# Loading a first-layer weight in two groups, deriving one sine table from the other, and one ring of PSUM banks in the set-up of a fused FFT and MLP-mixer kernel

## The chip, the cores and the metric

The kernel runs on one core of one Trainium2 chip. The metric is the device time of one execution in microseconds (us). One execution is also recorded by the profiler; its "span" runs from the first to the last instruction and is about 1.8 us shorter than the time of the same execution (609.8 against 611.57 us before the change).

Names used below: PE is the matrix engine, DVE the vector engine, ACT the scalar engine, POOL the engine that here issues most loads, SP the engine that issues stores and transposing DMAs. PEld, in the tables, is PE's loading of weights. PSUM is the memory that PE writes its products into. The "granted clock" is the share of full speed that the throttle lets PE run at.

## The reference, cut to what matters

```python
X = np.fft.fft(np.fft.fft(x, axis=1), axis=2).real        # x: 8 x 3008 x 256
xt = X.transpose(0, 2, 1)
h  = np.maximum(xt @ w_tok1, 0.0) @ w_tok2                 # token mixing, 3008 -> 256 -> 3008
u  = X + h.transpose(0, 2, 1)
out = u + np.maximum(u @ w_ch1, 0.0) @ w_ch2               # channel mixing, 256 -> 1536 -> 256
```

The kernel writes both Fourier transforms as products with sine tables that it generates itself. It folds the token transform into the first token weight once: the "carried" products hp and hq are w_tok1 multiplied by the transposed tables tp and tq. All batches then use hp and hq. So the set-up makes the tables, loads x of batch 0 and all the weights, and carries w_tok1 through the tables. After it comes a long steady part, 8 batches of 6 chunks.

## The kernel before: the parts that matter

The loads, all issued by POOL in this order: x of batch 0 (xp, xm), w_tok1 (w1p, w1m), w_tok2 (w2s), half of w_ch1 (wc1), later w_ch2 (wc2) and x of batch 1.

```python
    for i in range(2):                                   # w_tok1: four DMAs, 12 blocks each
        gdma(w1p[64 * i:64 * i + 64, :, :], dram(w1_t, ...))
        gdma(w1m[64 - 64 * i:128 - 64 * i, 0:NG - 1 + i, :], dram(w1_t, ...))
    w2s = const.tile([P, 2, S], FP16, tag="w2s")
    gdma(w2s[:], dram(w2_t, ...))
```

Each sine table is made from an angle reduced to one period: two ACTIVATEs (`near`) and one DVE operation (`rest_of`), then two sine ACTIVATEs (`table3`). The second table starts from its own angle, mq = mp + dq.

One carried product works on two blocks g, and reads both halves of the weight:

```python
    def carried(tts, dst, g2, e):
        ph = ps_mm("ph")
        for k in range(2):
            g = 2 * g2 + k
            o = ph[:, k * DTOK:(k + 1) * DTOK]
            nc.tensor.matmul(o, lhsT=tts[0][:, g * P:g * P + P], rhs=w1p[:, g, :],
                             start=True, stop=False)
            nc.tensor.matmul(o, lhsT=tts[1][:, g * P:g * P + P],
                             rhs=w1m[:, NG - 1 - g, :], start=False, stop=True)
        copy(e, dst[...], ph[:])          # e = 0: ACT, 1: DVE
```

PSUM has eight banks, kept in three pools: "mm" (3), "o2" (2) and "f" (3). The set-up interleaves three streams on PE, and the PE timelines below show them in this order (`own` yields eight groups of pz products and then twelve pw products of batch 0's transform):

```python
    take(own, 4)                         # the last four of the eight pz
    turn_rows(tts_p, 1.0, 0)             # "pr": rows of the first table reversed
    table3(tq, vq)                       # sines of the second table
    table_perm()
    take(own, 3)                         # pw 0 to 2
    carried(tts_p, hp, 0, 1)
    take(own, 2)
    carried(tts_p, hp, 1, 0)
    ...                                  # cut
    turn(tq, tts_q, 0)                   # "pt": the second table transposed
    ...                                  # cut: hp 3 to 5, hq 0 to 5, batch 0's token products
    filler(12)
    ...
        # steady part, first chunk; from batch 0's third step on:
                if b == 0 and 3 <= sub < 9:
                    take(early, 2)                       # fold of x of batch 1, on DVE
                    if sub == 8:
                        x_tiles[2] = load_x(2)
```

"pc" is the first product of the steady part (u times w_ch1). The time of the first pc marks the end of the set-up.

## Time and profile before

| | before |
|---|---|
| time, median of the runs beside the changed kernel (lowest to highest) | 611.77 us (611.5 to 613.0) |
| span of the profiled run, PE busy | 609.8 us, 97% |
| first pc | 38.56 us |
| PE waits for w1m | 2.15 us, until 21.64 us |
| granted clock between 21 and 25 us | 0.50 to 0.66 |

A kernel whose main engine is busy for 97% seems to leave little to gain. These are lines of the first two parts of its page: the span, busy time of PE, and then the span in 40 slices of about 15 us each, a digit being tenths of a slice.

```profile
span 609.8 us, 15701 instructions
...
PE 591.3 (97%) x6323; PEld 423.0 (69%) x6323; DVE 453.2 (74%) x1020; ACT 439.4 (72%) x986; POOL 147.8 (24%) x230
...
PE   5799999999999999999999999999999999999996
...
PEclk9899999999999999999999999999999999999999
```

PE is below 9 tenths only in the first two slices, some 30 us, and in the last, which this change does not touch. (The granted clock is below 9 in the second slice too.) A time by stretches shows the same: from 38.6 to 60 us PE is busy for 21.40 of 21.40 us. So only the first 38 us can give time back, as long as the change leaves the amount of steady work alone.

The chain of waits of the first 60 us (start, length, what; "issue" is time in which the engine waited for nothing that the profile shows), before the change:

```profile
6.33 0.86 POOL w1p L164
...
8.68 12.91 DMA w1m<-in_moe_w_tok_dram
21.59 0.04 issue
21.64 0.37 PE ph L403
```

The largest piece of the chain is 12.91 us in which the set-up depends on the last of the four w_tok1 loads. The PE timeline shows what that costs (start, length, engine, line of the program, operands, form, count; in brackets the idle time before it and who ended it):

```profile
17.17 0.23 PE L529 MATMUL pw<-tdu,z 128*128 128x128 f16 x1 [0.55 <-ACT z L288]
18.58 0.23 PE L529 MATMUL pw<-tdb,z 128*128 128x128 f16 x1 [1.18 <-DVE z L286]
...
19.22 0.27 PE L401 MATMUL ph<-w1p,tt 128*128 128x256 f16 x1
21.64 0.37 PE L403 MATMUL ph<-w1m,tt 128*128 128x256 f16 x1 [2.15 <-DMA w1m<-in_moe_w_tok_dram]
21.80 0.42 PE L401 MATMUL ph<-w1p,tt 128*128 128x256 f16 x1
...
36.72 1.33 PE L674 MATMUL pu<-w2s,uu 128*128 128x512 f16 x4 [0.73 <-ACT uu L605]
...
38.56 1.58 PE L714 MATMUL pc<-ut,wc1p 128*128 128x512 f16 x6
```

PE starts its first carried product at 19.22 us, because w1p is there, and stops at the second factor for 2.15 us. A stretch table of 1 us steps shows the other half of the cost (columns: window and its length; busy time of PE, PEld, DVE, ACT, POOL with counts; granted clock; DMA share; GB/s):

```profile
20.00:21.00 1.00, 0.00 (x0) 0.00 (x0) 0.06 (x1) 0.20 (x1) 1.00 (x3) 1.00 1.02 200
21.00:22.00 1.00, 0.36 (x2) 0.25 (x2) 0.00 (x0) 0.00 (x0) 0.50 (x2) 0.66 1.10 229
22.00:23.00 1.00, 1.00 (x11) 0.92 (x9) 0.53 (x1) 0.00 (x0) 0.39 (x1) 0.50 1.08 223
...
24.00:25.00 1.00, 1.00 (x11) 0.99 (x10) 0.01 (x1) 0.80 (x2) 0.00 (x0) 0.63 1.02 211
```

After the idle stretch, the clock is granted at half for about three microseconds. The ph products then start 0.21 us apart (21.80 to 22.02 us) instead of 0.11 us as later.

### The profile page before, as it was taken

The page shows a single profiled execution, that of the slowest core. Times are in us where ns is not written, and L with a number is a line of the kernel's source. Part 1 is how long each engine was busy: PE and PEld are TensorE (multiplying, and loading weights), DVE is VectorE, ACT ScalarE, POOL GpSimd, SP SyncE. Part 2 cuts the span into 40 slices and gives each one's busy share as a digit, 9 for nine tenths or more (in the row PEclk, how much of TensorE's full clock was granted, in tenths as well). Part 3 has the DMA queues.
Part 4 walks back from the last instruction along what each step waited for, and adds up shares of the span by engine and source line. Part 5 has one row for each costly group of instructions (what it writes and reads, how often), then busy time and mean ns, then how long its engine had stood idle before and what let it go on. Part 6 is the DMA issues. An engine that isn't in the chain of part 4 may idle for free.

```text
span 609.8 us, 15701 instructions
## 1 busy us (share of the span) xinstructions
PE 591.3 (97%) x6323; PEld 423.0 (69%) x6323; DVE 453.2 (74%) x1020; ACT 439.4 (72%) x986; POOL 147.8 (24%) x230
## 2 busy tenths in 40 slices
PE   5799999999999999999999999999999999999996
PEld 4566667666777678666777767766787667766675
DVE  8669679658987697757988689856979676676572
ACT  8666886677778777687777767777776877767772
POOL 8400413111143113401314212321131112111131
PEclk9899999999999999999999999999999999999999
DMA  9992953724538423682339333392231523232423
GB/s 153 209 185 81 185 75 59 152 50 85 67 74 153 90 53 68 115 125 53 78 63 168 61 81 77 64 185 58 53 68 45 100 53 78 64 70 59 90 58 100
DMA packets 86601, 56.53 MB, mean 93 GB/s; under 512 B 54864, under 2 KB 83472, under 8 KB 85776
## 3 DMA queue, kind: packets, MB, share of 16 engines
q1 hardware_dynamic: 78048, 37.84, 31.4%
q0 software_dynamic: 8256, 17.49, 16.6%
q8 instruction: 49, 0.80, 0.5%
q14 instruction: 24, 0.20, 0.1%
q10 hardware_dynamic: 224, 0.20, 0.1%
HBM read 34.98 MB, written 24.64 MB: 98 GB/s over the span
## 4 chain that ended last, share of the span: by engine, by line
PE 92%; DVE 3%; DMA 2%; ACT 1%; POOL 1%; issue 0%; DVEq 0%; POOLq 0%
PE pc L714 39%; PE px L755 23%; PE py L755 9%; PE pu L674 7%; PE po L812 4%; PE pt L582 4%; DMA w1m<-in_moe_w_tok_dram 2%; PE pz L486 1%; PE pq L614 1%; PE py L614 1%; PE pw L566 1%; PE pw L565 1%; DVE sb L731 1%; DVE w L568 1%; PE ph L403 0%; DVE osb L740 0%
## 5 line engine op out<-in xcount | busy, mean ns | idle before, releaser
L717 ACT ACTIVATE c<-pc 128x512 f16<-128x512 f32 (+1 forms) x572 | 295.8, 594 | 38.2 <-PE pc L714 20.6
L740 POOL TENSOR_TENSOR osb<-osb,rt 128x256 f32<-128x256 f32 x84 | 81.0, 964 | 381.3 <-DVE osb L740 364.8
L714 PE MATMUL pc<-ut,wc1p 128*128 128x512 f16 x576 | 140.5, 379 | 0.0
L755 PEld LDWEIGHTS <-c 128*128 128x128 f16 x2016 | 121.3, 98 | 20.7 <-issue 1.3
L714 PE MATMUL pc<-ut,wc1m 128*128 128x512 f16 (+1 forms) x576 | 134.8, 370 | 0.0
L682 DVE TENSOR_TENSOR ut<-pu,yt 128x512 f16<-128x512 f32 (+1 forms) x96 | 64.7, 674 | 52.9 <-PE pu L674 52.7
L755 PEld LDWEIGHTS <-sb 128*128 128x128 f16 x1512 | 89.9, 98 | 10.8 <-DVE sb L731 0.7
L760 ACT ACTIVATE m<-px 128x256 f32<-128x256 f32 x126 | 48.6, 386 | 66.9 <-PE px L755 41.9
L714 PEld LDWEIGHTS <-wc1p 128*128 128x128 f16 x576 | 52.2, 98 | 49.2 <-issue 2.6
L714 PEld LDWEIGHTS <-wc1m 128*128 128x128 f16 x576 | 53.0, 98 | 46.4
L755 PE MATMUL px<-wst,c 128*128 128x128 f16 x1008 | 70.8, 219 | 0.2 <-DVE c L731 0.2
L755 PE MATMUL px<-wc,c 128*128 128x128 f16 x1008 | 63.1, 219 | 0.0
L731 DVE TENSOR_TENSOR sb<-sb,c 128x768 f16<-128x768 f16 x84 | 50.3, 598 | 2.9
L288 ACT ACTIVATE z<-pz 128x480 f16<-128x480 f32 (+1 forms) x60 | 40.0, 671 | 16.9 <-PE pz L486 11.0
L740 DVE TENSOR_TENSOR osb<-py,m 128x256 f32<-128x256 f32 x84 | 35.2, 419 | 22.2 <-ACT m L760 17.4
L731 DVE TENSOR_TENSOR sb<-c 128x768 f16<-128x768 f16 x84 | 49.2, 586 | 2.4 <-ACT c L717 2.4
L674 PE MATMUL pu<-w2p,uu 128*128 128x512 f16 (+1 forms) x168 | 50.0, 379 | 0.0
L731 DVE TENSOR_TENSOR sb<-c,sb 128x768 f16<-128x768 f16 x84 | 47.1, 561 | 0.0
L731 DVE TENSOR_TENSOR c<-c 128x768 f16<-128x768 f16 x84 | 46.6, 554 | 0.0
L568 DVE SCALAR_TENSOR_TENSOR w<-alt,pw 128x131 f16<-128x131 f16 x84 | 29.4, 350 | 19.5 <-ACT w L288 18.9
L621 DVE TENSOR_TENSOR yt<-py,qs 128x512 f16<-128x512 f32 x48 | 30.9, 686 | 16.0 <-ACT qs L617 15.7
L755 PE MATMUL py<-wst,sb 128*128 128x128 f16 x504 | 35.2, 219 | 0.5 <-DVE sb L731 0.5
(186 smaller groups left out, 687.9 us busy)
## 6 DMA issues: line engine op xcount, KB each, us to landing
out_dram<-osb SPq DMA_DIRECT2D x83, 256.0 KB, 3.8
xp<-in_x_dram POOLq DMA_DIRECT2D x16, 272.0 KB
out_dram<-osb SPq DMA_DIRECT2D x11, 192.0 KB, 3.2
xp<-in_x_dram POOLq DMA_DIRECT2D x16, 127.5 KB
rt<-ut SPq DMA_TRANSPOSE x96, 3.5
w2s<-in_moe_w_tok_dram POOLq DMA_DIRECT2D x1, 1504.0 KB
w1p<-in_moe_w_tok_dram POOLq DMA_DIRECT2D x2, 384.0 KB
wc<-in_moe_w_ch_dram POOLq DMA_DIRECT2D x1, 768.0 KB
```

Of the source, the lines that this page charges most:

```text
L288: nc.scalar.activation(out=out_, in_=in_, func=AFT.Copy)
L568: nc.vector.scalar_tensor_tensor(out=w[:, g, 0:131], in0=alt[:], scalar=pw[:, 131:132], in1=pw[:, 0:131], op0=AT.mult, op1=AT.add)
L582: nc.tensor.matmul(pt[:, o:o + n], lhsT=hw[:, g, th * P:th * P + P], rhs=w[:, g, f:f + n], start=(g == 0), stop=(g == NG - 1))
L621: nc.vector.tensor_tensor(out=yt[:, h, CW * c:CW * c + CW], in0=py[:], in1=qs[:], op=op)
L674: nc.tensor.matmul(pu[:, 0:n], lhsT=uu[:, th, int(minus), h, :], rhs=w2_cols(b, c)[:, th], start=(th == 0), stop=(th == 1))
L682: nc.vector.tensor_tensor(out=ut[:, h, 0:n].rearrange("p (a b) -> p a b", b=64), in0=pu[:, 0:n].rearrange("p (b a) -> p a b", b=64), in1=y ...
L714: nc.tensor.matmul(pc[:, 0:n], lhsT=wc[:, h, ct * P:(ct + 1) * P], rhs=ut[:, h, 0:n], start=(h == 0), stop=(h == 1))
L717: nc.scalar.activation(out=c1[:, ct, 0:n], in_=pc[:, 0:n], func=AFT.Relu)
L731: nc.vector.tensor_tensor(out=o, in0=x, in1=y, op=op)
L740: eng.tensor_tensor(out=o, in0=x, in1=y, op=AT.add)
L755: nc.tensor.matmul(o[:, t], lhsT=a(k)[:, f:f + P], rhs=w(k), start=(first and t == 0 and k == 0), stop=(k == HC - 1), skip_group_check=True)
L760: nc.scalar.activation(out=m[:, i], in_=pa[:, 0], func=AFT.Copy)
```

## The change

The intent: begin the carried products with half of w_tok1 instead of waiting for all of it; make the second table available earlier and with less work on ACT; and let the set-up use all eight PSUM banks in turn, whatever stream asks. The diff, cut to its core:

```diff
+    ring = cycle((("f", 3), ("mm", 3), ("o2", 2), ("f", 3), ("mm", 3), ("f", 3), ("mm", 3),
+                  ("o2", 2)))
+    def ps_any(name, dt=FP32, n=512):
+        tag, bufs = next(ring)
+        return psum.tile([P, n], dt, tag=tag, name=name, bufs=bufs)
 ...   # pt, pr, fillers, ph, pz, pw and pt1 of the set-up take ps_any
-    for i in range(2):
-        gdma(w1p[64 * i:64 * i + 64, :, :], ...)
-        gdma(w1m[64 - 64 * i:128 - 64 * i, 0:NG - 1 + i, :], ...)
+    for g0, g1 in ((0, 6), (6, NG)):
+        for i in range(2):
+            gdma(w1p[64 * i:64 * i + 64, g0:g1, :], ...)
+            m0, m1_ = NG - g1, min(NG - g0, NG - 1 + i)
+            gdma(w1m[64 - 64 * i:128 - 64 * i, m0:m1_, :], ...)
 ...
-    nc.scalar.activation(out=mq[:], in_=mp[:], func=AFT.Identity, bias=dq[:])
+    nc.vector.scalar_tensor_tensor(out=vq[:], in0=vp[:], scalar=side[:], in1=vp[:],
+                                   op0=AT.mult, op1=AT.max)      # |vp| where side is -1
 ...   # four small DVE operations make side and the phase shifts; offq, dq and mq go
     warm(24)
-    near(vq, mq)
+    table3(tq, vq, (shift0[:], shift1[:]))
+    turn(tp, tts_p, 16)
     table_d()
     ...
-    rest_of(vq, mq, S)
 ...   # fillers, and which of ACT and DVE copies some products out of PSUM, change too
 ...   # order of the products after the folds of batch 0:
+    take(own, 3)
+    turned_out(tts_q, turn_in(tq))
+    for g2, e in enumerate((1, 1)):
+        carried(tts_p, hp, g2, e)
+    table_perm()
+    take(own, 4)
+    carried(tts_p, hp, 2, 0)
+    turn_rows(tts_q, -1.0, 0)
+    take(own, 3)
+    carried(tts_p, hp, 3, 1)
 ...
```

More of the change, by code (lines that the diff above doesn't have):

```diff
@@ L167 @@
     x_tiles = {0: load_x(0)}
-    icol, scol, gt32, eq32, mid, reff, offp, offq, tmp = (
+    icol, scol, gt32, eq32, mid, reff, offp, tmp = (
         pvec(n) for n in ("icol", "scol", "gt32", "eq32", "mid", "reff", "offp",
-                          "offq", "tmp"))
+                          "tmp"))
     ts(icol[:], pcol[:], 64.0, AT.is_ge)
@@ L189 @@
                                    op0=AT.mult, op1=AT.add)
-    nc.vector.scalar_tensor_tensor(out=offq[:], in0=mid[:], scalar=-752.0, in1=tmp[:],
-                                   op0=AT.mult, op1=AT.add)
-    for i in range(2):
-        gdma(w1p[64 * i:64 * i + 64, :, :],
-             dram(w1_t, i * DTOK, [[NQ * DTOK, 64], [2 * DTOK, NG], [1, DTOK]]))
-        gdma(w1m[64 - 64 * i:128 - 64 * i, 0:NG - 1 + i, :],
-             dram(w1_t, (25 - i) * DTOK,
-                  [[NQ * DTOK, 64], [2 * DTOK, NG - 1 + i], [1, DTOK]]))
+    for g0, g1 in ((0, 6), (6, NG)):
+        for i in range(2):
+            gdma(w1p[64 * i:64 * i + 64, g0:g1, :],
+                 dram(w1_t, (i + 2 * g0) * DTOK,
+                      [[NQ * DTOK, 64], [2 * DTOK, g1 - g0], [1, DTOK]]))
+            m0, m1_ = NG - g1, min(NG - g0, NG - 1 + i)
+            gdma(w1m[64 - 64 * i:128 - 64 * i, m0:m1_, :],
+                 dram(w1_t, (25 - i + 2 * m0) * DTOK,
+                      [[NQ * DTOK, 64], [2 * DTOK, m1_ - m0], [1, DTOK]]))
     w2s = const.tile([P, 2, S], FP16, tag="w2s")
@@ L238, in sin, with table3 @@
         nc.scalar.activation(out=out_, in_=in_, func=AFT.Sin, scale=PI2 / period)
-    def table3(tab, r):
+    def table3(tab, r, shift=(0.0, 0.0)):
         for i in range(2):
             nc.scalar.activation(out=tab[:, :, 64 * i:64 * i + 64], in_=r[:],
-                                 func=AFT.Sin, scale=half[i][:])
+                                 func=AFT.Sin, scale=half[i][:], bias=shift[i])
     def turned():
@@ L248, in turned, with turn_in @@
                 for _ in range(2)]
-    def turn(tab, tts, warm):
+    def turn_in(tab):
+        pts = []
         for h in range(2):
-            pt = psum.tile([P, 1024], FP16, tag="mm", name="pt", bufs=3)
+            pt = ps_any("pt", FP16, 1024)
             for g in range(6):
@@ L255, in turn, with turned_out @@
                                     in_=tab[:, 6 * h + g, :], identity=ident[:])
-            copy(0, tts[0][:, 768 * h:768 * h + 768], pt[:, 0:768])
+            pts.append(pt)
+        return pts
+    def turned_out(tts, pts):
+        for h in range(2):
+            copy(0, tts[0][:, 768 * h:768 * h + 768], pts[h][:, 0:768])
+    def turn(tab, tts, warm):
+        turned_out(tts, turn_in(tab))
         filler(warm)
@@ L260, in turn_rows @@
         for h in range(3):
-            pr = ps_mm("pr")
+            pr = ps_any("pr")
             nc.tensor.matmul(pr[:], lhsT=anti[:], rhs=tts[0][:, 512 * h:512 * h + 512],
@@ L272, in warm @@
     def warm(n):
-        pw = ps_out("filler")
+        pw = ps_any("filler")
         for _ in range(n):
@@ L278, in filler @@
     def filler(n):
-        pw = ps_mm("filler")
+        pw = ps_any("filler")
         for _ in range(n):
@@ L290 @@
     pl = nc.gpsimd
-    dq, r2, r47 = (pvec(n) for n in ("dq", "r2", "r47"))
-    nc.vector.tensor_tensor(out=dq[:], in0=offq[:], in1=offp[:], op=AT.subtract)
+    r2, r47 = (pvec(n) for n in ("r2", "r47"))
     ts(r2[:], reff[:], 2.0, AT.mult)
@@ L297 @@
     gp = gen.tile([P, NG], FP32, tag="gp")
-    mp, vp, mq, vq = (gen.tile([P, NG, 64], FP32, tag=n, name=n)
-                      for n in ("mp", "vp", "mq", "vq"))
+    mp, vp, vq = (gen.tile([P, NG, 64], FP32, tag=n, name=n)
+                  for n in ("mp", "vp", "vq"))
     ts(gp[:], jrow[:, 0:NG], r2[:], AT.mult, offp[:], AT.add)
@@ L321 @@
     ts(half[1][:], icol[:], PI2 / S, AT.mult)
+    quart, side, shift0, shift1 = (pvec(n) for n in ("quart", "side", "shift0", "shift1"))
+    nc.vector.tensor_tensor(out=quart[:], in0=gt32[:], in1=mid[:], op=AT.add)
+    ts(side[:], quart[:], -2.0, AT.mult, 1.0, AT.add)
+    for o, h in ((shift0, half[0]), (shift1, half[1])):
+        nc.vector.scalar_tensor_tensor(out=o[:], in0=h[:], scalar=-S / 4.0, in1=quart[:],
+                                       op0=AT.mult, op1=AT.mult)
     mask0, q24 = pvec("mask0"), pvec("q24")
@@ L394, with carried @@
     hq = const.tile([P, NG, DTOK], FP16, tag="hq")
-    def carried(tts, dst, g2, e):
-        ph = ps_mm("ph")
+    def carried(tts, dst, g2, e, pool=ps_any):
+        ph = pool("ph")
         for k in range(2):
@@ L513, in edge @@
                                  start=(i == 0), stop=(i == 1))
-        five = cycle((ps_f, ps_out, ps_f, ps_out, ps_f))
         for t0, e in Z0_ORDER:
@@ L518, in zw0 @@
                 if t0:
-                    inner(xp, t0, half, z_put(z, half, t0, e[half]), next(five))
+                    inner(xp, t0, half, z_put(z, half, t0, e[half]), ps_any)
                 else:
                     outer(xp, half, z_put(z, half, 0, e[half]), edge,
-                          next(five))
+                          ps_any)
                 yield
@@ L525, in zw0 @@
         for g in range(NG):
-            pw = next(five)("pw")
+            pw = ps_any("pw")
             for lo, hi in ((131, WD), (0, 131)):
@@ L536 @@
     Z0_ORDER = ((11, (0, 0)), (0, (1, 1)), (6, (0, 1)), (1, (0, 1)))
-    W0_COPY = [1] * 5 + [0, 1, 1, 1, 0, 1, 0]
+    W0_COPY = [1] * 7 + [0, 1, 0, 1, 0]
     def front(b):
@@ L857 @@
     own = zw0()
-    filler(8)
     take(own, 2)
-    turn(tp, tts_p, 8)
-    take(own, 2)
+    turn_rows(tts_p, 1.0, 0)
+    take(own, 3)
     table_b()
-    rest_of(vq, mq, S)
-    take(own, 4)
-    turn_rows(tts_p, 1.0, 0)
-    table3(tq, vq)
-    table_perm()
-    take(own, 3)
-    carried(tts_p, hp, 0, 1)
-    take(own, 2)
-    carried(tts_p, hp, 1, 0)
-    take(own, 2)
-    carried(tts_p, hp, 2, 1)
-    turn(tq, tts_q, 0)
-    take(own, 2)
-    carried(tts_p, hp, 3, 1)
+    take(own, 3)
[3 more added lines that the diff above has]
+    table_perm()
+    take(own, 4)
+    carried(tts_p, hp, 2, 0)
     turn_rows(tts_q, -1.0, 0)
     take(own, 3)
+    carried(tts_p, hp, 3, 1)
+    take(own, 3)
     carried(tts_p, hp, 4, 0)
+    take(own, 2)
     carried(tts_p, hp, 5, 1)
-    mirrored(state[0]["w"], ps_out("pt1"))
+    carried(tts_q, hq, 0, 0)
+    mirrored(state[0]["w"], ps_any("pt1"))
     own = front(0)
-    carried(tts_q, hq, 0, 0)
+    carried(tts_q, hq, 1, 1)
     take(own, 1)
-    carried(tts_q, hq, 1, 0)
-    carried(tts_q, hq, 2, 1)
+    carried(tts_q, hq, 2, 0)
     take(own, 1)
-    carried(tts_q, hq, 3, 0)
-    carried(tts_q, hq, 4, 1)
-    carried(tts_q, hq, 5, 0)
+    carried(tts_q, hq, 3, 1, ps_mm)
+    carried(tts_q, hq, 4, 0, ps_mm)
+    carried(tts_q, hq, 5, 0, ps_mm)
     take(own, 3)
```

## The prediction

> **What bounds it now.** The page: span 609.8 us, PE busy 97%. From 38.56 us on PE never idles (table of stretches: 5.00 of 5.00 us), so a gain must come from the set-up before. The timeline of PE shows there: scattered waits until the first "pw" product at 17.2 us; PE idle 2.15 us, released at 21.64 us by the DMA of w1m; then half clock (granted 0.50 to 0.66 between 21 and 25 us: "ph" steps at 0.21 us instead of 0.11), some 1.6 us lost; dense work to 36.0; 0.7 us wait for "uu"; pu, filler, first pc at 38.6. The chain of waits gives 12.91 us to the DMA of w1m (8.68 to 21.59 us). The Trainium skill's "TensorE: Matmul & The Clock Gate", Part 1, says an idle window of about 3.4 us halves the clock and a busy one restores it; the 3.3 us of half-rate steps agree.
>
> **What the change does.**
> 1. w1 in two groups: 4 more issues on POOL (0.85 us each, off PE's path), same bytes. From the GB/s by microsecond (about 200 KB each us; x of batch 0 is 1.6 MB, w1 1.5 MB), the first half should land at 17 to 18 us, the second at 21.6 to 22.2. Carried 0 to 2 and pw 0 to 6 then run while the second half arrives.
> 2. Second table: removed are three ACTIVATEs (0.92+0.94+0.94) and one vector op (1.04), added one vector op (about 1.0) and 4 small ones, ahead of the fold of x, which starts about 1.2 us later (12.2 instead of 10.95). The removed vector op stood before the last z copies, so these stay near 18.2 us (was 18.5). tq is ready near 12.4 instead of 20.2.
> 3. One ring of eight PSUM banks: fewer waits for evictions between pr, pw and ph.
>
> **Sum.** After: carried 0, 1 near 17.6 to 18.4 us, pw 0 to 3, carried 2, three pr, pw 4 to 6 till about 21.4; carried 3 at about 22, when the second half is in. Left then, at full clock (from the trace: pw 0.23 us, carried 0.43, third 0.44, tok1 2.7): 5x0.23 + 9x0.43 + 0.44 + 2.7 = 8.2 us, so tok1 ends at 30.2 to 30.6 (was 36.0). With the unchanged 0.7 us wait, pu and fillers the first pc starts near 33.0 instead of 38.6: 5.6 us gained. Next floor: wc1. POOL waited for w2s until 28.57 and for the first half of wc1 until 30.42; the gathered half should land near 32.4, so 6.2 us is about the most. Later, the fold of batch 1 (47.6 us before, about 42 after) comes close to the landing of its x (DMA rate falls at 43 us): DVE may wait 1 to 2 us, mostly absorbed by PSUM buffers; I take off 0.3 us.
>
> Predicted 606.7 us (-0.9%), 8 in 10 between 605.2 and 609.6. Faster by over 2%: 0.01; within 2%: 0.98; slower: 0.01.
>
> **What would show it.** Right: first ph before 18.5 us; no granted clock near 0.5 between 21 and 25; PE idle before w1's second half under 0.7 us; first pc near 33; from there the traces run in step. Wrong: half clock returns at 17 to 21 us, because PE is sparse between 13 and 18 us (costs up to 1.6); first half lands only with the second (gain under 3); first pc waits for wc1.
>
> **What would make it wrong.** Skewed DMA rings, so that groups land late; ACT as next limit (back to back from 14.5 to 22 us in my sum); gain given back near 42 us.

## The result and the profile after

| | before | after |
|---|---|---|
| time, median (lowest to highest), 4 runs each | 611.77 us (611.5 to 613.0) | 606.38 us (605.9 to 607.62) |
| ratio, 95% interval | | 0.9911 (0.9891 to 0.9931) |
| span of the profiled run | 609.8 us | 605.8 us |
| first pc | 38.56 us | 32.91 us |
| granted clock between 21 and 25 us | 0.50 to 0.66 | 1.00 |

A ratio is the mean time of one kernel's fast runs over the mean of the other's from the same rounds, so it is not quite the ratio of the medians. The interval lies clear of 1. The median fell by 5.4 us, against 5.2 us predicted from the earlier median (611.93 to 606.7).

The PE timeline of the changed kernel, to be held against the one above:

```profile
13.75 0.60 PE L509 MATMUL pz<-t1n,xp 94*128 94x96 f16 x10 [1.17 <-DVE xp L479]
...
17.48 0.27 PE L424 MATMUL ph<-w1p,tt 128*128 128x256 f16 x1
17.59 0.27 PE L426 MATMUL ph<-w1m,tt 128*128 128x256 f16 x1
...
21.04 0.27 PE L424 MATMUL ph<-w1p,tt 128*128 128x256 f16 x1
21.15 0.27 PE L426 MATMUL ph<-w1m,tt 128*128 128x256 f16 x1
...
31.07 1.33 PE L696 MATMUL pu<-w2s,uu 128*128 128x512 f16 x4 [0.73 <-ACT uu L627]
...
32.91 1.58 PE L736 MATMUL pc<-ut,wc1p 128*128 128x512 f16 x6
```

The first carried product (L424 is the w1p product, L426 the one with w1m) runs at 17.48 us without a wait. The first one that needs the second group is the one at 21.04 us, and it does not wait either. The first pc comes at 32.91 us, 5.65 us earlier. The stretches that had half clock now have all of it:

```profile
21.00:22.00 1.00, 1.00 (x18) 0.95 (x16) 1.00 (x4) 1.00 (x3) 0.80 (x3) 1.00 1.06 217
22.00:23.00 1.00, 1.00 (x18) 0.95 (x15) 0.81 (x2) 0.88 (x3) 1.00 (x2) 1.00 1.05 217
```

But the two profiled spans differ by only 4.0 us (609.8 to 605.8), not by 5.65. So something was given back after the first pc. The chain of waits shows it. Before the change PE alone carries it from 38 to 60 us; afterwards it contains these pieces:

```profile
30.12 15.43 DMA xm<-in_x_dram,ix
...
45.68 0.24 DVE xp L455
...
59.16 0.56 DVE sb L753
...
60.10 0.83 PE px L777 x12
```

The load of x of batch 1 (xm) lasts until 45.55 us. DVE, which now comes to the fold of batch 1 at about 42 us instead of 47.6 us, stood still for 3.7 us for it. Its timeline:

```profile
45.68 0.23 DVE L455 TENSOR_TENSOR xp<-xp,xm 94x16 f16<-94x16 f16 x1 [3.67 <-DMA xm<-in_x_dram,ix]
```

All that DVE does next comes later for it. The block sums "sb" that PE needs are then late: the last of them ends at 59.7 us (59.16 and its 0.56), one more DVE operation follows, and PE goes on with its px products at 60.10 us. The table of waits of PE says how long PE stood for it, in a window from 38 to 120 us (engine, line, who; us in total, times, longest):

```profile
PE py L777 <- DVE sb L753: 1.7, 2, 1.2
```

In the kernel before, the same group is 0.5 us, once. The profiled run was also the slowest of the four (607.62 us). One profile of each kernel therefore understates the gain by more than a microsecond.

### The profile page after: what moved, and what is told of

Read it like the earlier page. It is cut to its first block, busy times and chain, and to the rows that moved or that the text cites. A ratio compares the mean times of both kernels' runs of the same rounds, so it can differ in the third digit from the quotient of the medians.

```text
span 605.8 us, 15712 instructions
## 1 busy us (share of the span) xinstructions
PE 589.6 (97%) x6323; PEld 421.7 (70%) x6323; DVE 454.3 (75%) x1022; ACT 437.0 (72%) x983; POOL 148.5 (25%) x234
## 4 chain that ended last, share of the span: by engine, by line
PE 86%; DMA 6%; DVE 5%; issue 1%; ACT 1%; POOL 1%; DVEq 0%; POOLq 0%
PE pc L736 37%; PE px L777 23%; PE py L777 9%; PE pu L696 6%; PE po L834 3%; PE pt L604 3%; DMA xm<-in_x_dram,ix 3%; DMA w2s<-in_moe_w_tok_dram 2%; PE pz L509 1%; DMA w1p<-in_moe_w_tok_dram 1%; DVE sb L753 1%; PE pq L636 1%; PE py L636 1%; DVE osb L762 1%; DVE xp L457 1%
## 5 line engine op out<-in xcount | busy, mean ns | idle before, releaser
L590 DVE SCALAR_TENSOR_TENSOR w<-alt,pw 128x131 f16<-128x131 f16 x84 | 29.3, 350 | 18.2 <-ACT w L305 17.6
```

The lines of the kernel that those rows point to most:

```text
L590: nc.vector.scalar_tensor_tensor(out=w[:, g, 0:131], in0=alt[:], scalar=pw[:, 131:132], in1=pw[:, 0:131], op0=AT.mult, op1=AT.add)
```

## The experiments

The kernels ran in three series, each with its own runs of the kernel before (the texts call a series a batch; elsewhere "batch" is one of the eight of x). Two readings are used throughout: the first pc, and the span less the first pc, which is what happened after the set-up. All kernels gave correct results.

| kernel | time, us (median) | ratio to before (95%) | first pc | span | span less first pc |
|---|---|---|---|---|---|
| before | 611.77 | | 38.56 | 609.8 | 571.2 |
| after | 606.38 | 0.9911 (0.9891 to 0.9931) | 32.91 | 605.8 | 572.9 |
| a_again | 606.66 | 0.9909 (0.989 to 0.9928) | 33.59 | 605.2 | 571.6 |
| a_fold5 | 605.93 | 0.99 (0.9879 to 0.9922) | 32.89 | 604.0 | 571.1 |
| b_fold5 | 611.68 | 0.9993 (0.9971 to 1.0014) | 38.77 | 610.0 | 571.2 |
| b_fill | 610.72 | 0.9984 (0.9965 to 1.0003) | 37.07 | 608.1 | 571.0 |
| b_split | 607.41 | 0.9931 (0.9914 to 0.9947) | 34.19 | 605.3 | 571.1 |
| a_onegroup | 610.94 | 0.9987 (0.997 to 1.0004) | 37.91 | 609.1 | 571.2 |
| a_oldtable | 611.3 | 0.9987 (0.997 to 1.0004) | 39.16 | 610.3 | 571.1 |
| a_noring | 606.92 | 0.9917 (0.9902 to 0.9932) | 34.05 | 605.3 | 571.2 |
| f_again | 605.74 | 0.9892 (0.9876 to 0.9907) | 32.90 | 604.0 | 571.1 |
| f_noring | 607.06 | 0.9912 (0.9898 to 0.9925) | 34.08 | 605.3 | 571.2 |
| f_oldorder | 607.86 | 0.9925 (0.9911 to 0.9938) | 35.09 | 606.3 | 571.2 |
| f_three | 605.78 | 0.9892 (0.9876 to 0.9907) | 32.81 | 604.0 | 571.2 |

The last column is the most useful: it is 571.0 to 571.2 us in every profile but two, the two of the changed kernel as it stands. Everything else is decided before the first pc.

The theory: the gain is made in the set-up, mostly by the split, which takes away a wait and the half clock that follows it; part of it is given back where DVE runs into x of batch 1. Rivals are named with each run.

### The changed kernel again (a_again)

No edit; a yardstick.

> The changed kernel unchanged, as the yardstick of this batch. Theory: 605.8 to 607.6 us, first pc near 32.9 us in the profile; its runs scatter more than those of the kernel before, because DVE waits for x of batch 1 (3.7 us in the first profile) and PE loses 0 to 1.8 us at 57 to 60 us from it. Rival: no wait there, scatter of the whole chip.

Measured: 606.66 us (605.88 to 606.99, 5 runs). First pc at 33.59 us: this time PE waited 0.41 us at 18.15 us for w1m of the first group, so this load lands on the edge of being needed. DVE waited 2.2 us for x of batch 1, and the part after the first pc was 571.6 us, some 0.4 us longer than the usual. The two losses trade: the later the set-up ends, the later DVE comes to the fold, and the less it waits. That is only about half of the difference in DVE's wait, though: x of batch 1 also landed 0.8 us earlier here (the fold began at 44.92 instead of 45.68 us), and no run shows why. The expected first pc near 32.9 us was missed by 0.7 us, which is what the late first group cost (nearly 0.6 us) and a second short wait, of 0.1 us, for w1m of the second group at 21.82 us.

### The fold of batch 1 two steps later (a_fold5, b_fold5)

```diff
-                if b == 0 and 3 <= sub < 9:
+                if b == 0 and 5 <= sub < 11:
                     take(early, 2)
-                    if sub == 8:
+                    if sub == 10:
                         x_tiles[2] = load_x(2)
```

> The changed kernel with the fold of batch 1 (and the load of batch 2 behind it) two steps later. Theory (DVE runs into x of batch 1, its backlog makes the block sums late, PE waits 1.45 us for sb and osb at 57.7 to 60.1 us): DVE's wait of 3.7 us goes, the py wait of 1.2 us goes, first pc stays at 32.9, span near 604.1, time 605.3 to 606.0, narrower than the unchanged one. Rival (the backlog is not the cause; late transposes of u or the bus are): the py wait stays and the time does not change.

> The kernel before with the same later fold: a control. Theory: x of batch 1 has landed at about 45.6 us, the fold runs at 47.6 us, so nothing waits and the time stays at 611.5 to 612.0. Rival (the later fold is simply a better order): faster by about 1 us here too.

DVE timeline of the changed kernel with this edit (a_fold5), around the fold:

```profile
47.79 0.22 DVE L455 TENSOR_TENSOR xp<-xp,xm 94x16 f16<-94x16 f16 x1
...
55.27 0.55 DVE L753 TENSOR_TENSOR sb<-c 128x768 f16<-128x768 f16 x1
```

DVE comes to the fold (L455) at 47.79 us and no longer waits for a load; the sum sb that was late in the changed kernel (there it started at 58.58 us) starts at 55.27 us. In the table of waits of PE for a_fold5, again from 38 to 120 us, the wait for sb is back at what the kernel before has:

```profile
PE py L777 <- DVE sb L753: 0.5, 1, 0.5
```

The span less the first pc is 571.1 us. The time is 605.93 us (605.76 to 606.05), and the mean of its runs is 0.7 us below that of the unedited changed kernel in the same series of runs (605.92 against 606.60). In the kernel before, the same edit changes nothing that its interval could tell (0.9971 to 1.0014). So the later fold is not a better order in itself; it removes a loss that the faster set-up created. This is the best version, repeated in the last series (605.74 us, 605.72 to 605.91): it beats both kernels, the changed one by some 0.7 us or 0.1% in the series that has both; there the fastest of the unedited runs (605.88 us) lies within the range of the edited ones.

### Filling the idle stretch before the first carried product (b_fill)

In the kernel before:

```diff
     take(own, 3)
+    filler(36)
     carried(tts_p, hp, 0, 1)
```

> The kernel before with 36 filler products (about 2.0 us) where PE waits for w1, nothing else. Theory (the idle stretch costs twice, 2.15 us of waiting and then 3.3 us at half clock): first ph with w1m still at about 21.6 us, but ph steps of 0.11 us from the start and no granted clock of 0.5, first pc near 37.0 instead of 38.6, time near 610.2. Rival (the slow ph steps come from loading or from late operands, not from idleness): steps stay 0.21 us, time 611.8.

PE timeline of b_fill, from the fillers on:

```profile
19.22 2.17 PE L281 MATMUL filler<-ident 128*128 128x128 f16 x36
21.23 0.27 PE L401 MATMUL ph<-w1p,tt 128*128 128x256 f16 x1
21.64 0.27 PE L403 MATMUL ph<-w1m,tt 128*128 128x256 f16 x1
21.74 0.27 PE L401 MATMUL ph<-w1p,tt 128*128 128x256 f16 x1
...
37.07 1.58 PE L714 MATMUL pc<-ut,wc1p 128*128 128x512 f16 x6
```

PE still gets w1m at 21.64 us, to the hundredth. But the next ph products follow 0.11 us apart, the clock is 1.00 in every microsecond from 13 to 30, and the first pc comes at 37.07 us, 1.49 us earlier. So the slow products were slow because PE had been idle, and the half clock cost about 1.5 us in this profile on top of the wait. (The Trainium skill, "TensorE: Matmul & The Clock Gate", Part 1, has the clock fall to half after an idle window of about 3.4 us. This run agrees on the cause, but not on the length: in the kernel before, 2.15 us of standing still were enough.) The time is less clean: 610.72 us median with runs of 609.86 to 612.16 and an interval up to 1.0003. Two of the six runs had a mean clock of 0.993 and 0.997, and were the longer ones of 611.88 and 612.16 us; the four of 0.998 to 1.000 took 609.86 to 611.14 us. Fillers thus did not keep the clock up in each run. What differed in those two runs has not been profiled.

### The split alone (b_split)

In the kernel before, only the loop that loads w_tok1 is replaced by that of the change; the order of products stays.

```diff
-    for i in range(2):
-        gdma(w1p[64 * i:64 * i + 64, :, :], ...)
-        gdma(w1m[64 - 64 * i:128 - 64 * i, 0:NG - 1 + i, :], ...)
+    for g0, g1 in ((0, 6), (6, NG)):
+        for i in range(2):
+            ...                                   # as in the change
```

> The kernel before with w1 in two groups and nothing else (order of products unchanged). Theory: the first carried product goes on at 19.3 us without a wait, no half clock, first pc at 34.8 instead of 38.6 (gain 3.7 us: 2.15 of waiting and 1.6 of half clock), time near 608.1. Rival (first half lands only with the second): as before, 611.8. Rival (all parts are needed together): gain under 1 us.

PE timeline of b_split, the first pw products that had all z, the two first carried products of the two groups, and the first pc:

```profile
18.01 0.23 PE L532 MATMUL pw<-tdb,z 128*128 128x128 f16 x1 [0.70 <-DVE z L289]
...
18.65 0.27 PE L404 MATMUL ph<-w1p,tt 128*128 128x256 f16 x1
18.76 0.27 PE L406 MATMUL ph<-w1m,tt 128*128 128x256 f16 x1
...
22.00 0.27 PE L404 MATMUL ph<-w1p,tt 128*128 128x256 f16 x1
...
34.19 1.58 PE L717 MATMUL pc<-ut,wc1p 128*128 128x512 f16 x6
```

The first carried product (L404) has no wait, nor has the first that needs the second group (22.00 us). There is no half clock. The time is 607.41 us, so the split by itself brings 4.6 us (611.99 us for the kernel before in that series) of the 5.4. It is 0.7 us more than expected. The surplus is in front of the carried products: DVE's fold of x began at 10.46 us instead of 10.95, the last z copy came earlier, and the pw products that had all z began at 18.01 us instead of 18.58 us.

### The rest without the split (a_onegroup)

In the changed kernel, the loop is put back to one group of four DMAs.

```diff
-    for g0, g1 in ((0, 6), (6, NG)):
-        for i in range(2):
-            ...
+    for i in range(2):
+        ...                                       # as in the kernel before
```

> The changed kernel with w1 in one group again. Theory: PE stops at the first carried product (17.5 us) until w1 is in at about 21.6 us, and half clock follows for some 3 us; first pc near 38.0, time 611 to 612: without the split the rest is worth nearly nothing. Rival (the other parts carry half of the gain): 609.

PE timeline of a_onegroup, from the first carried product on:

```profile
18.93 0.28 PE L421 MATMUL ph<-w1p,tt 128*128 128x256 f16 x1 [1.09 <-DMA w1p<-in_moe_w_tok_dram]
20.95 0.36 PE L423 MATMUL ph<-w1m,tt 128*128 128x256 f16 x1 [1.74 <-DMA w1m<-in_moe_w_tok_dram]
21.11 0.42 PE L421 MATMUL ph<-w1p,tt 128*128 128x256 f16 x1
...
37.91 1.58 PE L733 MATMUL pc<-ut,wc1p 128*128 128x512 f16 x6
```

PE stands twice, 1.09 and 1.74 us, until 20.95 us, and the following ph products are 0.21 us apart again: half clock, 0.50 in each of the stretches from 21 to 24 us. First pc at 37.91 us as expected (38.0); time 610.94 us, about 1 us under the kernel before, with an interval that just includes 1. The rest of the change is thus worth little while w_tok1 is late. (The new table alone and the ring alone, each in the old order, were not run.)

### The old second table in the changed order (a_oldtable)

In the changed kernel, mq, dq and offq return, and with them the three ACTIVATEs and the DVE operation; the order of products stays.

```diff
-    table3(tq, vq, (shift0[:], shift1[:]))
+    near(vq, mq)
     turn(tp, tts_p, 16)
 ...
     table_b()
+    rest_of(vq, mq, S)
     take(own, 3)
+    table3(tq, vq)
     turned_out(tts_q, turn_in(tq))
```

> The changed kernel with the second table made in the old way (three ACTIVATEs and a vector op more, its two sines just before its transposes). Theory: ACT is back to back from 9 to 19 us, so tq comes near 20.8 us, PE stands with it at the transposes ahead of the first carried product, then half clock: first pc 3.5 to 4.5 us later, time near 610. Rival (the table is off the path): under 0.7 us lost.

PE timeline of a_oldtable, from the transposes of the second table on:

```profile
20.16 1.46 PE L265 MATMUL pt<-ident,tq 128*128 128x128 f16 x12 [2.70 <-ACT tq L252]
21.41 0.42 PE L420 MATMUL ph<-w1p,tt 128*128 128x256 f16 x1
...
39.16 1.58 PE L732 MATMUL pc<-ut,wc1p 128*128 128x512 f16 x6
```

The transposes of tq wait 2.70 us for its sines, until 20.16 us, what follows them on PE comes later too, and half clock reaches from 16 to 26 us (0.50 in each of the ten stretches of 1 us). The first pc is at 39.16 us, 6.2 us later and not the expected 3.5 to 4.5, later even than in the kernel before; the time is 611.3 us. Nearly all the gain is gone although the split is in. The wait is the expected one, but the half clock is not just its consequence, as the expectation had it: it begins at 16 us, before PE stops at about 17.5 us. Before it PE had been sparse (busy 0.12 us of the stretch from 13 to 14 us and 0.68 of the next), because its "pr" products waited for ACT; this is the danger that the prediction lists under "Wrong", though no run tests it alone. Nor does the run say that the table's saved work is worth 4.6 us. The order asks for the table early; it could not stand without it. That is why f_oldorder was run.

### Without the ring (a_noring, f_noring)

In the changed kernel, and then in the one with the later fold, the set-up's tiles return to their pools: pt, pr, ph and the fillers on ident to "mm", pz and pw to "f" and "o2" by turns.

```diff
-            pt = ps_any("pt", FP16, 1024)
+            pt = psum.tile([P, 1024], FP16, tag="mm", name="pt", bufs=3)
-            pr = ps_any("pr")
+            pr = ps_mm("pr")
-    def carried(tts, dst, g2, e, pool=ps_any):
+    def carried(tts, dst, g2, e, pool=ps_mm):
 ...   # fillers, pz, pw, pt1 likewise
```

> The changed kernel with the PSUM pools of the kernel before in place of the one ring. Theory: the ring matters little, PE waits for an evicted bank in a few places: first pc 0 to 0.7 us later, time 606.3 to 607.1. Rival (three mm banks hold up pr, ph and the transposes together): over 1.5 us lost.

> The later fold, with the PSUM pools of the kernel before in place of the one ring. The run without the ring gave a first pc 1.1 us later (34.05) than expected, but hardly a longer time, because DVE then waited less for x of batch 1. Theory: with the later fold nothing hides it: first pc at 34.0, time 606.9 to 607.1, 1.1 us over the yardstick. Rival (the 1.1 us was the late first half of w1, not the ring): first pc 32.9 to 33.6, time as the yardstick.

a_noring looked like a success of the expectation in time (606.92 us against 606.3 to 607.1) and was a miss in the profile: the first pc was at 34.05 us, 1.1 us late, not 0 to 0.7. The time hid it, because with a later set-up DVE waited only 1.2 us for x of batch 1 and PE lost nothing to it (571.2 us after the first pc). With the later fold there is nothing to hide it behind: 607.06 us against 605.74 us for f_again in the same series, 1.3 us, about as expected. PE timeline of f_noring, the second carried product and the first pc:

```profile
18.69 0.27 PE L424 MATMUL ph<-w1p,tt 128*128 128x256 f16 x1 [1.17 <-ACT tt L305]
...
34.08 1.58 PE L737 MATMUL pc<-ut,wc1p 128*128 128x512 f16 x6
```

The first carried product ran at 16.92 us without a wait. The second does not read the second table either, yet it waits 1.17 us for ACT's copy of that table's transposes. By the program's order, what the copy gives it is the bank: the two pt and the first ph fill the three "mm" banks, and the second ph needs the first pt's. The ring spreads them over eight. So the ring is worth about 1.2 us in this order.

### The old table in an order that suits it (f_oldorder)

The later fold, the old table, and tq's transposes moved behind carried 0 to 2 and seven pw; its reversed rows behind carried 3 and three more pw.

```diff
     table3(tq, vq)
-    turned_out(tts_q, turn_in(tq))
     ...                                  # carried 0, 1; pw 0 to 3
     carried(tts_p, hp, 2, 0)
-    turn_rows(tts_q, -1.0, 0)
     take(own, 3)
+    turned_out(tts_q, turn_in(tq))
     carried(tts_p, hp, 3, 1)
     take(own, 3)
+    turn_rows(tts_q, -1.0, 0)
     carried(tts_p, hp, 4, 0)
```

> The later fold, the second table made in the old way, but its transposes moved behind seven pw and three carried products, and its reversed rows behind carried 3 and three more pw. Theory (the 4.6 us lost without the new table came from the order, which puts its transposes ahead of the first carried product): no stop of PE and no half clock, first pc 33.0 to 33.8, time 606.0 to 606.8, so that the table by itself is worth under 0.9 us. Rival (the ACTIVATEs it saves are what counts): first pc after 35, time over 608.

PE timeline of f_oldorder, the first carried product and the first pc, and a stretch of 1 us in the form used above:

```profile
17.37 0.37 PE L420 MATMUL ph<-w1p,tt 128*128 128x256 f16 x1
...
35.09 1.58 PE L732 MATMUL pc<-ut,wc1p 128*128 128x512 f16 x6
...
18.00:19.00 1.00, 1.00 (x6) 0.70 (x5) 1.00 (x3) 1.00 (x3) 0.72 (x4) 0.50 1.45 195
```

PE no longer stands for tq, as the theory had it, but half clock came back, and the theory fell: the first pc came at 35.09 us, as the rival had it (after 35), and the time was 607.86 us, 2.1 us over f_again; the theory had allowed 0.9 us, and the rival's "over 608" was missed narrowly. The carried product begins at 17.37 us, no later than in the changed kernel (17.48), but at half clock: the granted clock was 0.83 in the stretch of 16 to 17 us and 0.50 from 17 to 20. Not all of it is the clock: the two of the five runs whose mean clock was 0.998 and 1.000 still took 607.50 and 607.71 us. The new table is thus worth about 2 us, if this is a good order for the old one; other orders were not tried. In the profiled run most of the 2.2 us can be counted: from the first carried product to the third PE took 3.08 us, at half clock, where f_again took 1.78, and then tq's transposes, some 0.7 us, which f_again had behind it by then, were still to come. As the two runs with the higher clock were hardly faster, the division need not be the same in them; no profile shows it. The run also shows that the parts do not add up: split, ring and old table together (607.86 us) are no faster than the split alone (607.41 us, in another series).

### Three groups (f_three)

```diff
-    for g0, g1 in ((0, 6), (6, NG)):
+    for g0, g1 in ((0, 4), (4, 8), (8, NG)):
```

> The later fold, with w1 in three groups of four, an attempt at a better version. Theory: carried 0 and 1 need only the first third, which lands about 1.3 us earlier (a sixth of 1.5 MB at 0.2 MB a us), so the wait of 0.4 us seen there in one profile can't occur: first pc 32.5 to 32.9, time 605.4 to 605.9. Rival (four more issues hold POOL up, and w2s and wc1 with it): first pc later than 33.5, time over 606.3.

Measured: 605.78 us (605.73 to 605.82), first pc 32.81 us. The yardstick of the same series has 605.74 us. The wait of 0.41 us did not occur in the yardstick's profile, so there was nothing to take away; four more issues on POOL did no harm either. Two groups are enough.

## Why the prediction was right, point by point

The time lay 0.3 us from the number, and the first pc at 32.91 us was 0.1 us from its forecast. The mechanism (the wait and the half clock behind it go) is shown by the runs; that the number is so close is partly luck, as two of the steps below say. The steps:

- **"PE idle 2.15 us ... then half clock ... some 1.6 us lost"**: shown. b_fill removes the half clock alone and gains 1.49 us in its profile; b_split removes both. What the one profile does not show is that the lost clock varies from run to run: of the 31 runs of the kernel before beside these experiments, 18 had a mean clock of 0.994, with a mean span of 610.8 us, and 12 had 0.996 or 0.997, with 609.5 us (one had 0.993 and 609.9 us). The profiled run had 0.996. The changed kernel had 0.998 to 1.000 in all nine of its runs. So in most runs the set-up probably gained more than the two profiles show; that the clock is lost in the set-up in those runs too is not shown, as none with 0.994 was profiled.
- **"The first half should land at 17 to 18 us"**: right. The first carried product ran at 17.48 us without a wait in one profile, and in the repeat it waited until 18.15 us.
- **"The second at 21.6 to 22.2"**: too late for this profile, where the products that need it ran from 21.04 us without a wait; right for the repeat, where w1m was waited for until 21.82 us. The sum let the rest of PE's work begin with it, at about 22 us; it began 1.0 us earlier.
- **"Fold of x ... starts about 1.2 us later (12.2 instead of 10.95)"**: 11.68 us; the z copies ended at 18.0 us, against "near 18.2". tq's sines ran from 10.65 to 12.58 us, against "near 12.4".
- **"tok1 ends at 30.2 to 30.6"**: 30.34 us (start of the last group, 29.38, and its 0.96 us). The end was right because two misses cancelled, which is luck: the rest of PE's work began 1.0 us earlier than the sum had it, at 21.04 us, and took 9.3 us instead of 8.2. The two groups of tok1 products (25.79 to 27.16 us and 28.47 to 30.34 us) took 3.2 us instead of 2.7, as they had in the kernel before, and about 0.5 us passed before the pq products at 24.89 us, with PE waiting for ACT's copy of w; the sum had no such wait.
- **"One ring ... fewer waits"**: I gave it no size. It is 1.2 to 1.3 us (f_noring), in this order.
- **The split as the main part**: I summed the parts without saying which carries how much. Alone, the split gives 4.6 us; table, ring and order without it about 1 us; on top of it, with the later fold, about 1.5 us more (607.41 against 605.93 us, from two series).
- **"DVE may wait 1 to 2 us, mostly absorbed ...; I take off 0.3 us"**: the mechanism was right, the size only on the mean. DVE waited 3.7 us in the first profile and PE lost 1.7 us (572.9 less 571.2), 2.2 us and 0.4 us in the second, 1.2 us and nothing in a_noring. So a wait of 1.2 us was absorbed, and of what went beyond it PE lost 1.7 us of 2.5 in one profile and 0.4 us of 1.0 in the other. The 0.3 us stood on no working; that it fits the mean of the runs is luck. "From there the traces run in step" was wrong for the first profile.
- **"Next floor: wc1"**: the first pc never came before 32.81 us; no profile shows PE waiting for wc1, so this floor remains untested.

## What to carry to other kernels

When a large load gates a chain of small products, split it in the order of use and put the products of the first part where the second part is still under way; the return is the wait plus whatever clock PE loses by standing still. A faster start then brings every later consumer closer to loads that have not become faster: look for the next operation, on any engine, that used to come just after its load had landed, and move it back. And compare the stage that changed and the rest separately (here the first pc and what follows it), because a gain in one can hide a loss in the other, as the run without the ring did.

## What the Trainium skill lacked or had wrong

- "TensorE: Matmul & The Clock Gate", Part 1: the window of about 3.4 us agrees with the time at half clock here (granted 0.66, 0.50, 0.50 and 0.63 in four stretches of 1 us, which works out to 3.4 us at half). But the page has the clock fall after an idle window of that length, and here PE stood for only 2.15 us and had been busy for 0.42 and 0.49 us of the two stretches before (18 to 20 us). The page calls the phase of the window variable for a kernel's start. That the same holds for a gap in the middle of a set-up would fit the runs of the kernel before, but is not shown: 18 of 31 runs had a mean clock of 0.994 and took 1.3 us longer than the 12 with 0.996 or 0.997 (spans 610.8 and 609.5 us). With fillers in the gap, four of six runs had a mean clock of 0.998 to 1.000, not all.
- "DMA: Bandwidth & Descriptors", section "Anatomy of one DMA — SWDGE (gpsimd) path", does not say how POOL's issues queue behind one another. Here POOL sat 6.2 us at an issue of xm until w2s had landed (3.7 us in the changed kernel), and in the changed kernel it waited 0.8 and 1.2 us for x of batch 0 within the issues of w_tok1. Each time the DMA waited for was the eighth before the one to be issued. Whether the chip or the program sets this eight, no run shows.
- The same page's cost per DMA does not say which side's bytes count in a load that converts. The loads here turn 32-bit data into 16-bit, and moved about 200 GB/s counted in what was written (185 GB/s over the first 40 us of the kernel before); counted in what was read that would be twice as much.
- "SBUF — State Buffer", section "Who interferes with whom", lists `tensor_scalar` among the operations that can contend with POOL, when its operands meet the conditions for a two-port mode. That would fit an observation here that no run isolates: the same DVE operation (anti) took 0.62 us beside POOL's w_tok1 issues of 0.85 to 0.89 us in the kernel before, and 0.34 us beside issues of half the size (0.75 to 0.79 us) in b_split, whose fold of x began 0.5 us earlier (10.46 against 10.95 us). The page mentions a slower DVE beside POOL's own operations, but gives no size for DVE held up beside POOL's DMA issues; one would have let the prediction count it.
